# Half of a filter's rows transposed by DMA instead of on TensorE, with a new order of the work

## The chip, the cores and the metric

The kernel runs on one core of one Trainium2 chip. The metric is the device time of one execution in microseconds (us). A core has five engines that run side by side and wait for one another through semaphores: TensorE (PE in the profile; PEld are its weight loads), VectorE (DVE), ScalarE (ACT), GpSimd (POOL) and SyncE (SP). SP and ScalarE also issue DMAs, each into a queue of its own, and 16 DMA engines serve them.

## What is computed

Sequence length S = 2048, width D = 512, inner width 1792, all in bf16. In short:

```
xn = layernorm(A_q)                                  # over the 512 columns
kv = causal_shift_conv(A_k, A_shift_k, 4 taps) * A_v
y  = irfft(rfft(pad(kv)) * rfft(pad(A_ssm_k)))[:S] + kv * A_ssm_D      # a long convolution along the sequence
s  = xn * y
h  = gelu(xn @ w_gate) * (xn @ w_up)
g  = silu(h @ w_down)
out = A_q + s * g
```

A_ssm_k is the filter: 512 rows (one for each column of the sequence) of 2048 taps.

## The kernel before

**The parts of the work.** The layer norm works on 16 row tiles of 128 rows, four to a quarter q = 0 to 3 (`ln`, L809): statistics on VectorE (L811, L812), the power on GpSimd (L821, L822), the normalisation to XN on VectorE (L825). XN is transposed to xnT, for q = 0 and 1 on TensorE (L844, then a copy out of PSUM), for q = 2 and 3 by one DMA transpose each, issued by SP (L836). The gated product runs in units (`unit`, L1065): for quarter q and block m of 14, a gate piece (4 matmuls of 512 columns with Wg) and an up piece (4 with Wu), GELU on ScalarE (L1093), product HT on VectorE (L1096). The down products (`down`, L1099) follow with Wd. Nearly all matmuls go through one helper, L609.

**The long convolution** is a Fourier transform in two stages by matmul. Stage 1 multiplies with the table F1 along the 128 partitions; the result is staged in SBUF, written to a DRAM scratch (ZH for the filter, ZK for kv) and read back in another order (BH, BK) for stage 2, which works in blocks of 32x32 (L984). The products of the two spectra go through the inverse (ZI, BI, "y"). The filter reaches stage 1 like this: its 512 rows are loaded in four pieces h0 to h3 of 128 rows into Hn; `h_transpose` (L860) turns each piece by eight TensorE transposes of pairs of bf16 taken as fp32 (L868), in two halves of four, and ScalarE or VectorE copies each half to HTr; VectorE adds A_ssm_D to the first row (`h_fold`, L882); `stage1` (L905) multiplies, eight steps u = 0 to 7 of 512 columns twice (for u of 4 and more the first of them in halves of 256 columns, `half1`, L895, so that it can begin before h2 and h3 are there). The staging of stage 1 lies in free parts of XN and X, and ScalarE issues the eight stores to ZH, 512 KB each.

**The shift convolution** of A_k (`kshift`, L944) is a chain on VectorE, four rounds of eight operations over 128x2048 elements (L961, L965, L967, L969); each round ends with kv in V. Before it, GpSimd spreads the taps (SKB, L942).

**What sets the order.** All of this is cut into numbered tasks, in the order in which the code creates them. A list written out by hand, SEQ (L27), names every task once, and the instructions are emitted in just this order: on each engine and in each DMA queue, work is done in the order of the list. Semaphore waits come from the tracker (`Trk`, L82), where tiles overlap. The planner's constants (`Sched`, L292: durations, landing times) only choose PSUM banks and staging slots. ORDER (L26) is the order in which the load tasks are created; the order in which SP issues them is again that of SEQ. Gate and up tiles together hold at most four PSUM banks (NF_BANKS, L51). TensorE begins with 11 matmuls on zeros (`warm_up`, L665).

Read through the numbering, SP issues the loads in this order before the change: x rows 0 and 1 of the 16 row tiles (256 KB), h0, h1, x rows 2 and 3, first gate weights, first up weights, h3, second gate weights, x rows 4 to 7, h2, halo of A_k, second up weights, taps, last weights, k0, last up, third weights, k1, v0, both halves of Wd, v3, k2, v2, k3, v1. The weights come in pieces for m = 0 and 1, 2 to 5, 6 to 9, 10 to 13.

Of the kernel before, what the change touches and what calls it, by code (L numbers as in the profile page):

```python
# [14 lines left out]
DM = 512  # L15
# [10 lines left out]
ORDER = "x00 h0 h1 x01 w0 w1 h2 h3 D0 w2 s0 k0 v0 x1 w3 k1 v1 d0 d1 k2 v2 k3 v3 x2 x3"  # L26
SEQ = (  # L27
    "0 2 3 5 4 7 17 18 6 11 1 8 9 12 10 66 19 67 68 74 20 69 75 50 21 49 52b 13 22 76 83 87b 77 54 56b 132 51 84 133 53 70 88 71 55 125 113 111 134 "
    "135 78 126 72 362 370 26 73 112b 79 372 371 363 364 127 85 80 61 81 86 62 23 373 36 365 14 15 96 452 446 450 448 25 89 90 31 97 64 128 114 447 "
    "453 449 451 378 390 366 374 376 392 368 382 375 58 367 454 60 377 369 16 57 386 115 24 30 384 59 63 388 391 383 387 455 458 393 385 456 457 389 "  # L30
    "380 116 142 141 379 459 129 32 381 37 34 130 33 27 38 131 418 414 422 140 139 416 424 143 420 463 144 65 145 461 136 460 415 417 146 28 39 29 "
    "419 410 137 98 138 464 412 465 117 99 423 402 101 406 421 100 102 408 407 398 462 35 41 42 46 43 44 147 151 148 425 409 149 394 411 400 466 91 "
    "399 413 92 404 152 401 395 118 93 396 119 94 467 103 120 403 121 469 104 45 40 153 397 154 405 155 106 495 491 468 108 497 107 493 105 109 150 "
    "156 122 471 496 511 223 470 123 95 513 224 218 512 499 159 157 498 160 514 161 225 441 442 443 492 158 162 219 110 124 494 220 226 473 501 82 "
    "233 500 436 437 475 163 502 164 167 227 48 177 221 477 234 235 438 483 236 165 228 426 485 222 237 229 47 175 176 230 231 427 476 168 166 243 "
    "169 478 244 170 245 428 246 171 479 238 444 239 481 172 472 474 507 240 173 429 439 509 174 431 430 440 432 445 433 253 232 247 183 178 241 434 "
    "254 242 255 508 510 256 487 257 489 248 249 488 250 515 637 435 490 179 251 180 252 188 480 503 484 181 182 184 258 505 639 635 640 633 636 638 "
    "482 634 185 545 546 543 641 504 519 186 643 644 544 506 642 486 645 520 516 521 517 271 528 189 523 529 284 190 193 187 518 522 259 260 263 524 "
    "530 646 547 549 548 191b 261 262 192 198 297 272 276b 273 533 525 285 264 550 289 265 526 531 534 286b 535 266 551 267 269 536 270 268 538 527 "
    "274 532 553 552 555 554 275 537 539 194 540 541 195 659 196 661 663 664 556 665 667 660 277 287 542 278 288 662 290 669 279 282 280 651 668 675 "  # L40
    "291 310 197 292 203 666 653 283 295b 670 293 647 655 298 649 302 657 299b 656 648 705 650 658 199 677 200 652 573 201 575 296 294 565 676 202 "
    "323 654 709 678 593 311 574 566 300 312b 576 301 303 315 567 204 595 205 206 577 594 304 561 568 596 305 306 609 308b 611 610 579 563 612 313 "
    "601 603 562 578 324 602 695 208 207 314 564 316 307 309 281 325 328 317 604 580 697 569 326 327 209 210 211 329 581 570 597 330 571 599 318 321 "
    "572 319b 598 585 336 213 349 212 331 334 587 600 583 557 696 332b 698 337 582 558 341b 333 338 322 559 339 560 340 586 214 683 588 584 342 343 "
    "320 215 605 606 607 335 216 685 699 217 589 608 344 345 701 591 347b 590 684 686 592 350 613 691 346 354 348 693 671 614 351b 352 623 672 615 "
    "353 355 356 673 357 358 713 717 674 360b 359 618 700 619 624 625 620 616 361 626 621 617 622 627 711 723 628 629 692 694 702 740 630 679 680 631 "
    "632 721 712 687 724 681 703 714 682 725 689 726 707 733 704 719 715 706 688 708 710 768 741 720 734 730 727 716 778 690 772 722 718 742 747 731 "
    "748 749 728 776 770 732 774 773 779 769 735 754 750 743 755 756 761 736 729 762 771 777 744 775 751 752 753 763 737 757 745 738 746 739 758 759 "
    "764 765 766 760 767 "
# [3 lines left out]
LOAD_NS = {("x0_", 262144): 800.0, 262144: 850.0, 524288: 1350.0, ("x", 524288): 2100.0, ("h", 524288): 1400.0, ("wg", 524288): 1550.0, ("wu", 524288): 1450.0, 917504: 2620.0, ("sk", 524288): 1500.0, 344064: 1250.0, 46080: 350.0, 3072: 100.0, 1024: 200.0}  # L53
# [238 lines left out]
class Sched:  # L292
# [8 lines left out]
    FIRST = {"loads": 300.0, "SP": 30500.0}  # L301
    DRAIN = 121.0
    EARLY, TAKEN, SHARED, WAIT = (2500.0, 1.6), 1400.0, 46000.0, 3300.0
    LANDS = (3850.0, 5450.0, 7050.0, 8650.0, 9600.0, 10450.0)
# [94 lines left out]
def build_kernel(nc, A_q, A_k, A_v, A_shift_k, A_ssm_k, A_ssm_D, B_w_gate, B_w_up, B_w_down, out):  # L399
    with ExitStack() as es0:  # L400
# [19 lines left out]
        X = new("X", [128, NT, DM], BF16)  # L420
        XN = new("XN", [128, NT, DM], BF16)
# [35 lines left out]
        HTr = at("HTr", [128, NT // 2, 2 * DM], BF16, kk_at - 16384)  # L457
# [21 lines left out]
        ast = {"H": [T[:, 4 * j:4 * j + 4, :].rearrange("p (r c) d -> p r c d", c=2) for T in (XN, X) for j in (2, 3)], "K": [AST[:, j, :, :, :] for j in range(2)] + [ASX[:]]}  # L479
# [48 lines left out]
        R_AST = {x: [res(f"AST{x}{j}", a) for j, a in enumerate(ast[x])] for x in "HK"}  # L528
# [9 lines left out]
        R_HTr = [[res(f"HTr{t}_{k}", HTr[:, t, 256 * k:256 * (k + 1)]) for k in range(KD)] for t in range(NT // 2)]  # L538
# [17 lines left out]
        R_Z = {"H": [trk.free_res(f"ZH{t}") for t in range(NT // 2)],  # L556
# [9 lines left out]
        pAST = {x: Pool_("AST" + x, len(ast[x])) for x in "HK"}  # L566
# [57 lines left out]
        bHTr = [[B(f"HTr{k}_{h}") for h in range(2)] for k in range(KD)]  # L624
# [4 lines left out]
        bZ = {x: [B(f"Z{x}{i}") for i in range(16 if x == "I" else 8)] for x in "HKI"}  # L629
# [134 lines left out]
        def load_x0(t, ring):  # L764
            load(f"x0_{t}", X[:, 2 * t:2 * t + 2, :], x_dr[:, 2 * t:2 * t + 2, :], R_X[2 * t:2 * t + 2], bX[0][2 * t:2 * t + 2], 262144, ring)

# [32 lines left out]

        for what in ORDER.split():  # L800
            if what[0] in "xa" and len(what) == 3:
                load_x0(int(what[2]), "SP" if what[0] == "x" else "ACT")
                continue
            {"k": load_k, "v": load_v, "w": load_w, "x": load_x, "d": load_wd, "h": lambda i: load_h(i, "SP"), "s": load_taps, "D": load_d}[what[0]](int(what[1:]))
# [4 lines left out]
        def ln(q):  # L809
# [3 lines left out]
            for h in range(1 if q else 4):  # L813
# [10 lines left out]
                for t in range(ts.start, ts.stop):  # L824
                    op([("DVE", 420.0)], lambda e, hd, t=t: hd.tensor_scalar(XN[:, t, :], X[:, t, :], mv[:, t, 0:1], mv[:, t, 3:4], ALU.subtract, ALU.mult),  # L825
                       r=[bX[q][t % 4], b], w=[bXN[t]], rr=[R_X[t], R_mv[t]], ww=[R_XN[t]])
# [51 lines left out]
        for k in range(KD):  # L878
            h_transpose(k)
# [25 lines left out]
        def stage1(x, u, Z):  # L905
            a = B(f"A{x}{u}", pAST[x])
            af = [] if x == "H" else s1_tasks["H"] + kshift_tasks[:1] + [t_table]
            for i in range(2):
                if x == "H" and i == 0 and u >= 4:
                    for k in range(2):  # L910
                        half1(u, k, a)
# [331 lines left out]
```

## Time and profile before

| | us |
|---|---|
| median of 3 runs | 196.24 |
| lowest, highest | 195.81, 196.43 |
| span of the profiled execution, first to last instruction | 193.8 |
| around the span, by the median | 2.4 |

The profile's own execution has only its span on the page; what lies around it is taken from the median of the runs. Of the span, DMA reads of HBM are 27.4 MB and writes 14.7 MB. The costliest groups are the gate, up and down matmuls (55.5, 55.8 and 52.7 us); the 32 transposes of the filter (L868) have 5.0 us of modelled, overlapping time.

How to read the lines that follow: in a timeline, the first number is the start in us, the second the length, then the engine, the line, the operation, what it writes and reads, and how many; in brackets stands how long the engine had been idle and what ended that. Matmuls are pipelined: one of 512 columns is listed with 379 ns, but the next starts 216 ns later. Engine names with a q (SPq) are issuing instructions.

### The profile page before, as it was taken

Reading aid. Unit: us, or ns where it says so; the run is one execution under the profiler, and the core shown is the slowest. Engines: PE = TensorE matmul, PEld = TensorE weight load, DVE = VectorE, ACT = ScalarE, POOL = GpSimd, SP = SyncE. Lnnn points to the kernel's source line nnn. Section 1 sums busy time; section 2 is a strip of 40 time slices with the busy share of each in tenths; the row PEclk is TensorE's granted clock in tenths of the full one; section 3 lists DMA queues with packets and bytes.
Section 4 is the critical chain, followed back from the end, with each engine's and each line's share of the span. In section 5 each row is a group of like instructions: output and inputs, shape, how many; then the busy total and the mean of one; then the engine's idle time right before and its main releaser. Section 6 shows DMA issues by size and latency. Waiting matters only on the chain.

```text
span 193.8 us, 3522 instructions
## 1 busy us (share of the span) xinstructions
PE 189.6 (98%) x1393; PEld 87.0 (45%) x1393; DVE 160.6 (83%) x246; ACT 120.7 (62%) x168; POOL 12.6 (7%) x32
## 2 busy tenths in 40 slices
PE   7999999999999999999999999999999999999993
PEld 2777444444444444443334334343344444444442
DVE  6998899899989797987996697887796871579984
ACT  5789877598794797874578666668656622150031
POOL 5322400000000000020200000000000000000000
PEclk9999999999999999999999999999999999999999
DMA  6999999999575659999999927788244305938643
GB/s 177 335 376 300 357 376 392 405 386 368 239 222 164 211 142 288 386 296 278 305 326 208 318 88 230 260 276 271 110 166 162 108 3 171 369 88 278 231 166 108
DMA packets 34502, 48.14 MB, mean 248 GB/s; under 512 B 8499, under 2 KB 27191, under 8 KB 34486
## 3 DMA queue, kind: packets, MB, share of 16 engines
q1 hardware_dynamic: 28982, 39.53, 63.1%
q10 hardware_dynamic: 5504, 8.39, 11.8%
q8 instruction: 11, 0.18, 0.4%
q14 instruction: 5, 0.04, 0.1%
HBM read 27.39 MB, written 14.68 MB: 217 GB/s over the span
## 4 chain that ended last, share of the span: by engine, by line
PE 94%; DVE 2%; DMA 2%; POOL 0%; ACT 0%; issue 0%
PE psall L609 86%; PE psall L984 5%; DMA X<-in_A_q_dram 2%; PE psall L868 1%; PE psall L844 1%; DVE XN L825 0%; DVE stats L811 0%; DVE HTr L603 0%; POOL mv L822 0%; DVE G L1131 0%; DVE G L1130 0%; ACT G L1128 0%; DVE xnT L603 0%; POOL mv L821 0%; DVE mv L812 0%
## 5 line engine op out<-in xcount | busy, mean ns | idle before, releaser
L609 PE MATMUL psall<-xnT,Wu 128*128 128x512 bf16 (+1 forms) x232 | 55.8, 372 | 0.0
L609 PE MATMUL psall<-xnT,Wg 128*128 128x512 bf16 (+1 forms) x232 | 55.5, 372 | 0.0
L609 PE MATMUL psall<-Wd,HT 128*128 128x512 bf16 (+2 forms) x238 | 52.7, 367 | 0.0
L1096 DVE TENSOR_TENSOR HT<-psall,GE 128x512 bf16<-128x512 f32 x54 | 36.2, 684 | 11.9 <-PE psall L609 10.9
L1093 ACT ACTIVATE GE<-psall 128x512 bf16<-128x512 f32 x54 | 31.2, 601 | 11.3 <-PE psall L609 9.0
L609 PEld LDWEIGHTS psall<-Wd,HT 128*128 128x128 bf16 x238 | 22.1, 98 | 26.2 <-issue 1.9
L609 PEld LDWEIGHTS psall<-xnT,Wg 128*128 128x128 bf16 x232 | 22.1, 98 | 25.8 <-issue 1.8
L609 PEld LDWEIGHTS psall<-xnT,Wu 128*128 128x128 bf16 x232 | 21.9, 98 | 25.7 <-issue 2.1
L600 ACT ACTIVATE HS<-psall 128x1024 bf16<-128x1024 f32 x15 | 14.7, 1022 | 5.2 <-PE psall L984 5.2
L600 ACT ACTIVATE BO<-psall 128x1024 bf16<-128x1024 f32 x10 | 10.0, 1023 | 10.6 <-PE psall L984 10.5
L600 ACT ACTIVATE KB<-psall 128x1024 bf16<-128x1024 f32 x10 | 10.0, 1023 | 7.7 <-PE psall L984 7.7
L965 DVE TENSOR_TENSOR KTM<-KK,SKB 128x2048 bf16<-128x2048 bf16 x12 | 14.6, 1214 | 0.1
L967 DVE TENSOR_TENSOR KAC<-KAC,KTM 128x2048 bf16<-128x2048 bf16 x12 | 14.6, 1213 | 0.0
L600 ACT ACTIVATE AST<-psall 128x1024 bf16<-128x1024 f32 x12 | 12.1, 1021 | 2.4 <-PE psall L609 2.1
L1120 ACT ACTIVATE G<-psall 128x512 bf16<-128x512 f32 x12 | 7.0, 599 | 10.4 <-PE psall L609 9.9
L1122 DVE SCALAR_TENSOR_TENSOR G<-G,psall 128x512 bf16<-128x512 bf16 x12 | 7.9, 683 | 6.3 <-ACT G L1120 6.3
L1047 DVE TENSOR_TENSOR HS<-KB,HS 128x1024 bf16<-128x1024 bf16 x16 | 10.8, 683 | 1.1 <-ACT KB L600 1.0
L603 DVE CAST BO<-psall 128x1024 bf16<-128x1024 f32 x6 | 7.3, 1225 | 5.3 <-PE psall L984 5.2
L1128 ACT ACTIVATE G<-psall 128x512 bf16<-128x512 f32 (+2 forms) x5 | 2.5, 511 | 14.1 <-PE psall L609 14.1
L811 DVE BATCH_NORM_STATS2 stats<-X 128x6 f32<-128x512 bf16 x16 | 10.4, 675 | 0.7 <-DMA X<-in_A_q_dram 0.7
L1047 DVE TENSOR_TENSOR HW<-KB,HW 128x1024 bf16<-128x1024 bf16 x16 | 10.8, 682 | 0.0
L600 ACT ACTIVATE XN<-psall 128x1024 bf16<-128x1024 f32 (+1 forms) x10 | 8.4, 856 | 2.9 <-PE psall L609 2.8
(81 smaller groups left out, 179.4 us busy)
## 6 DMA issues: line engine op xcount, KB each, us to landing
BH<-ZH SPq DMA_DIRECT2D x8, 512.0 KB, 5.8
HW<-HS SPq DMA_DIRECT2D x16, 256.0 KB, 3.0
BK<-ZK SPq DMA_DIRECT2D x8, 512.0 KB, 5.9
ZI<-BO ACTq DMA_DIRECT2D x16, 256.0 KB, 2.5
BI<-ZI SPq DMA_DIRECT2D x8, 512.0 KB, 4.5
ZK<-AST SPq DMA_DIRECT2D x6, 512.0 KB, 3.0
Hn<-in_A_ssm_k_dram SPq DMA_DIRECT2D x4, 512.0 KB, 6.4
KK<-in_A_k_dram SPq DMA_DIRECT2D x4, 512.0 KB, 10.8
```

Source lines behind the costliest of these rows:

```text
L600: return h.activation(o, i, ACTF.Copy, scale=scale)
L603: return h.tensor_copy(o, i)
L609: return h.matmul(o, lhsT=l, rhs=r, start=st, stop=sp)
L811: t_stats[t] = op([("DVE", 670.0)], lambda e, h, t=t: h.bn_stats(stats[:, t, :], X[:, t, :]), r=[bX[q][t % 4]], w=[bst[t]], rr=[R_X[t]], w ...
L965: op([("DVE", dur)], lambda e, h, j=j, m=m: h.tensor_tensor(KTM[:, m.slot, :, :], kk(j), sk(j), ALU.mult), r=need + [bSKB[j], a], w=[m], r ...
L967: op([("DVE", dur)], lambda e, h, m=m: h.tensor_tensor(KAC[:, a.slot, :, :], KAC[:, a.slot, :, :], KTM[:, m.slot, :, :], ALU.add), r=[m], ...
L984: trk.op("PE", lambda h: h.matmul(ps(s, i)[b, :], lhsT=wt(col)[a, :], rhs=data(col)[a, :], start=n < 16, stop=n >= len(todo) - 16, tile_po ...
L1047: return hd.tensor_tensor(o, flat(KB, kb[h]), o, ALU.mult)
L1093: op([("ACT", act(512))], lambda e, h: h.activation(GE[:, g.slot, :], bank(pg), ACTF.Gelu_apprx_tanh), r=[pg], w=[g], rr=lambda: R_bank(pg ...
L1096: op([("DVE", dve(512, 1))], lambda e, h: h.tensor_tensor(HT[:, q % 2, m, :], bank(pu), GE[:, g.slot, :], ALU.mult), r=[pu, g], w=[bHT[q][m]],
L1120: op([("ACT", act(n))], lambda e, h, g=g, pc=pc: h.activation(g, pc(), ACTF.Tanh, scale=0.5), r=[p], w=[bt], rr=lambda p=p: R_bank(p), ww= ...
L1122: op([("DVE", dve(512, 1))], lambda e, h, g=g, pc=pc: h.scalar_tensor_tensor(out=g, in0=g, scalar=1.0, in1=pc(), op0=ALU.add, op1=ALU.mult ...
```

## The change

Rows 256 to 511 of the filter (h2, h3) are no longer turned on TensorE. GpSimd copies them, in four pieces of 128x1024, into HP so that the taps of one stage-1 column lie together; two DMA transposes, issued by SP, then write HTD. HTr shrinks to h0 and h1. Stage 1 of the filter is split by the source: "H" from HTr, "J" from HTD, each with eight steps of 2 matmuls of 512 columns (H still in halves for u of 4 and more). Each has its staging (now in X, and for J also in G) and its eight stores to ZH, of 256 KB with runs of 512 bytes; ScalarE issues those of H, SP those of J. The fold of A_ssm_D is split likewise, 256 columns on HTr and 256 on HTD. Some waits follow from where the new tiles lie: HP and HTD use space of HT, XN and a staging tile.

The first load of x is cut: rows 0, 1 and then 2 and 3. SEQ is new from end to end, and so are some constants of the planner. Read through the numbering, SP issues now: x row 0, x row 1, h0, x rows 2 and 3, first gate weights, first up weights, h1, second gate weights, x rows 4 to 7, second up weights, halo, third gate and up weights, A_ssm_D, taps, k0, h2, k1, last gate and up weights, h3, v0, v3, **DMA transpose 0, DMA transpose 1**, k2, both halves of Wd, v1, a table transpose (MI), k3, v2. The list gives GpSimd its copies in the order h2 (half 1), h2 (half 0), h3 (half 0), h3 (half 1). VectorE begins: statistics of row 0, of row 1, normalisation of row 0, statistics of row 2, normalisation of row 1. TensorE begins: warm-up, eight transposes of h0, first transpose of xn, a stage-1 half, second transpose of xn, three stage-1 halves, first gate and up halves (m = 1), third transpose of xn, a gate half (m = 0), fourth transpose of xn, four transposes of h1, an up half, four transposes of h1, the first wide gate (m = 3). Stage 1 of "J" comes later, between gate, up and down pieces of the first two quarters.

```diff
-ORDER = "x00 h0 h1 x01 w0 w1 h2 h3 D0 w2 s0 k0 v0 x1 w3 k1 v1 d0 d1 k2 v2 k3 v3 x2 x3"
+ORDER = "x01 h0 x11 h1 x22 w0 w1 h2 h3 D0 w2 s0 k0 v0 x1 w3 k1 v1 d0 d1 k2 v2 k3 v3 x2 x3"
...
-    FIRST = {"loads": 300.0, "SP": 30500.0}
+    FIRST = {"loads": 1050.0, "SP": 30500.0}
...
-        HTr = at("HTr", [128, NT // 2, 2 * DM], BF16, kk_at - 16384)
+        HTr = at("HTr", [128, NT // 2, DM], BF16, kk_at - 16384)
+        HP = at("HP", [128, NT, 2, 128], BF16, kk_at - 8192)
+        HTD = at("HTD", [128, NT, 2, 128], BF16, xn_at + 8 * 1024)
...
+        ast = {"H": [quarter(X, j) for j in (8, 10, 12, 14)], "J": [quarter(T, j) for T, j in ((X, 12), (X, 14), (G, 4), (G, 6))],
...
-        def load_x0(t, ring):
-            load(f"x0_{t}", X[:, 2 * t:2 * t + 2, :], x_dr[:, 2 * t:2 * t + 2, :], R_X[2 * t:2 * t + 2], bX[0][2 * t:2 * t + 2], 262144, ring)
+        def load_x0(t, n, ring):
+            load(f"x0_{t}", X[:, t:t + n, :], x_dr[:, t:t + n, :], R_X[t:t + n], bX[0][t:t + n], 131072 * n, ring)
...
-        for k in range(KD):
+        for k in range(2):
             h_transpose(k)
+        h_perm, h_dtr = [], []
+        d_htd = [dsem(f"d_htd{hf}") for hf in range(2)]
+        for hf in range(2):
+            for k in range(2):
+                h_perm.append(op([("POOL", 1250.0)], lambda e, h, hf=hf, k=k: h.tensor_copy(HP[:, 8 * hf:8 * hf + 8, k, :], Hn[:, 2 + k, :].rearrange("p (a t) -> p t a", t=NT)[:, 8 * hf:8 * hf + 8, :]),
+                                 r=[bHn[2 + k]], w=[bHP[hf]], rr=[R_Hn[2 + k]], ww=[R_HP[hf]]))
+        for hf in range(2):
+            def dtr(e, hf=hf):
+                o = HTD[:, 8 * hf:8 * hf + 8, :, :].rearrange("p t k d -> p (t k) d")
+                trk.dma("SP", lambda h: h.dma_start(out=o, in_=HP[:, 8 * hf:8 * hf + 8, :, :].rearrange("p t k a -> p (t k a)"), transpose=True), d_htd[hf], r=[R_HP[hf]], w=[R_HTD[hf]])
+            h_dtr.append(S.add([("loads", 4500.0)], dtr, r=[bHP[hf]], w=[bHTD[hf]], nbytes=W_XT))
...
-        h_fold = op([("DVE", 420.0)], lambda e, h: h.tensor_tensor(HT0, HT0, Drow[:], ALU.add),
-                    r=[bHD, *[bHTr[k][0] for k in range(KD)]], w=[bFold], rr=[R_D, *R_HTr[0]], ww=R_HTr[0])
+        op([("DVE", 420.0)], lambda e, h: h.tensor_tensor(HT0, HT0, Drow[:, 0:256], ALU.add),
+           r=[bHD, *[bHTr[k][0] for k in range(2)]], w=[bFold], rr=[R_D, *R_HTr[0]], ww=R_HTr[0])
+        op([("DVE", 420.0)], lambda e, h: h.tensor_tensor(HD0, HD0, Drow[:, 256:512], ALU.add),
+           r=[bHD, bHTD[0]], w=[bFoldD], rr=[R_D, R_HTD[0]], ww=[R_HTD[0]])
...
+        def stage1_h(x, u):
+            a = B(f"A{x}{u}", pAST[x])
+
+            def st(e):
+                dst = bass.AP(ZH, 4 * u * DM + (256 if x == "J" else 0), [[32 * DM, 128], [DM, 4], [1, 256]])
+                dma(e, dst, ast[x][a.slot].rearrange("p r c d -> p (r c) d"), d_ast[x][a.slot], [R_AST[x][a.slot]], [R_Z["H"][u + (8 if x == "J" else 0)]])
...
+                if x == "H":
+                    data, rd, bd = HTr[:, u, :], R_HTr[u], [bHTr[k][u // 4] for k in range(2)] + ([bFold] if u == 0 else [])
+                else:
+                    data, rd, bd = HTD[:, 2 * u:2 * u + 2, :, :].rearrange("p t k d -> p (t k d)"), [R_HTD[u // 4]], [bHTD[u // 4]] + ([bFoldD] if u == 0 else [])
...
+            zh_tasks[x].append(S.add([("ACT", 350.0) if x == "H" else ("SP", ISSUE)], st, r=[a], w=[bZ["H"][u + (8 if x == "J" else 0)]], nbytes=1.05 * SMALL))
...
-        for t in x_late:
-            S.behind(t, zh_tasks)
+        S.behind(x_late[0], zh_tasks["H"])
+        S.behind(x_late[1], zh_tasks["H"] + zh_tasks["J"])
...
-            af = (down_tasks[q - 2] if q >= 2 else []) + (s1_tasks["H"] if q == 1 else [])
+            af = (down_tasks[q - 2] if q >= 2 else []) + ((s1_tasks["H"] if m < 8 else h_dtr) if q == 1 else [])
```

The new SEQ, a list of 788 task numbers, is told above as far as the text needs it.

## The prediction

> **What bounds the kernel now.** I read the page first: the busy shares, then the slices.
>
> ```profile
> span 193.8 us, 3522 instructions
> ...
> PE 189.6 (98%) x1393; PEld 87.0 (45%) x1393; DVE 160.6 (83%) x246; ACT 120.7 (62%) x168; POOL 12.6 (7%) x32
> ...
> PE   7999999999999999999999999999999999999993
> ...
> DMA  6999999999575659999999927788244305938643
> ```
>
> TensorE (PE) has work in every slice but the first and the last, so the time is its start, plus its work, plus its gaps. The DMA engines are full in slices 1 to 9 (5 to 48 us), while the inputs come in. The chain of waits is TensorE alone from 8.02 to 190.03 us, and it shows the pieces that the change takes out (columns: start, length, what):
>
> ```profile
> 11.97 0.49 PE psall L868 x4
> ...
> 12.69 0.50 PE psall L868 x4
> ...
> 17.52 0.44 PE psall L868 x4
> ...
> 18.40 0.44 PE psall L868 x4
> ```
>
> These are the filter's transposes of h3 and h2. The time outside the span is 196.24 - 193.8 = 2.4 us (2.0 to 2.6 by the three runs); I keep it, so changes of the span are added to the median, 196.24. What this measurement can tell from no change is 0.3%, 0.6 us.
>
> **The change part by part.**
>
> *Transposes gone.* The four groups above: 0.49 + 0.50 + 0.44 + 0.44 = **-1.87 us** on the chain. The stage-1 multiplications of the filter keep their number and widths, so nothing else leaves TensorE. Four evictions of 1.02 us (ScalarE, L600 HTr) go too, and two of 0.68 us move from VectorE to ScalarE. Neither is on the chain: ScalarE is busy 62%.
>
> *New order of the first loads.* The new order gives x row 0, x row 1, h0, x rows 2 and 3, the first gate and up weights, and only then h1. By the landing records of the trace, before has x rows 0 and 1 at 4.35, h0 at 5.59, h1 at 6.87, x rows 2 and 3 at 8.42, the weights at 9.35 and 10.20 us. The bytes up to h0 are the same, so the first transposes again start near 5.7. Rows 2 and 3 took 1.55 us behind h1, and a weight piece of the same size 0.93: they land between 6.5 and 7.2, I take 7.0. There is a catch on VectorE: in the new list the statistics of row 2 stand ahead of the normalisation of row 1, so that one waits for 7.0, then 0.70 (statistics) and 0.41 (L825), and ends at 8.1. The second transpose of xn so starts at about 8.15:
>
> ```profile
> 5.64 1.16 PE L868 MATMUL psall<-ident,Hn 128*128 128x128 f32 x8
> ...
> 8.02 0.40 PE L844 MATMUL psall<-ident,XN 128*128 128x128 bf16 x4
> ```
>
> Before has it at 8.02 and has by then also done four transposes of h1, which after can't have: 0.13 + 0.45 (four at the 0.44 to 0.50 above) = 0.58 lost. Against this, before stops weight loads 0.25 us at 13.38 for the ScalarE copy of the fourth xnT; in the new order rows 2 and 3 come earlier and that copy is done. Net **+0.33 us** (bounds 0 and 1.0). Later weights: up to k0, loads land at 3.15 us per MiB (4.35 to 23.62 us, 6.1 MiB), so the new order brings the weights of the first wide gate, its up and the next pair at about 11.4, 14.6 and 17.2 us. TensorE's work by the rows' lengths reaches them at 12.2, 15.2 and 19.5. Covered, by 0.6 us at the tightest; before's tightest is 0.47 (12.99 landed, 13.46 used).
>
> *GpSimd copies.* Four copies 128x1024. The nearest row is four of 128x512:
>
> ```profile
> 20.79 2.42 POOL L942 COPY SKB<-SKR 128x512 bf16<-128x512 bf16 x4 [2.08 <-DMA SKR<-in_A_shift_k_dram]
> ...
> 22.50 1.17 DVE L825 TENSOR_SCALAR XN<-X,mv 128x512 bf16<-128x512 bf16 x2
> ```
>
> That is 0.605 each, so 1.21 for twice the width and 4.8 us in all, on an engine that is otherwise idle. But look at VectorE's L825: the first of the two took 0.847 (the line's median is 0.409) while the last copy ran; VectorE lost 0.44. The reverse is seen too:
>
> ```profile
> 95.37 0.66 DVE L1047 TENSOR_TENSOR HW<-KB,HW 128x1024 bf16<-128x1024 bf16 x1
> ...
> 95.54 0.58 POOL L821 TENSOR_SCALAR mv<-mv 128x4 f32<-128x4 f32 x1 [11.76 <-DVE mv L812]
> ```
>
> L821 takes 0.24 elsewhere, here it ends 0.09 behind the VectorE operation. So the two hold each other up. By position the copies run from 24 to 33 us (h2 lands at 23.7, h3 near 30), beside the shift chain of L961 to L969, which fills VectorE with operations that read two tiles in SBUF; in before no copy ran beside that chain. Bounds: 0 and 4 x 1.21 = 4.8 us lost on VectorE; I take the row's 0.44 four times, 1.8 us. Who waits: behind the chain stand the HT products (L1096), which free the banks of TensorE. What lag is allowed?
>
> ```profile
> 30.57 1.03 PE L609 MATMUL psall<-xnT,Wu 128*128 128x512 bf16 x4
> ...
> 34.56 1.27 DVE L1096 TENSOR_TENSOR HT<-psall,GE 128x512 bf16<-128x512 f32 x2
> ```
>
> The first of these two products belongs to those four matmuls, and ends at 35.2, 3.6 us behind them, with TensorE not waiting. In the new order the shift chain starts near 23 (before: 24.79), and adding 1.135 per chain operation and 0.605 per product (the steps between their starts in this stretch) puts the products 2.1 to 2.5 us behind without any block. 3.6 - 2.4 = 1.2 us are to spare, so TensorE loses 1.8 - 1.2 = **+0.6 us** (0 to 3.6).
>
> [...]
>
> *The two DMA transposes.* Same shape as xnT's:
>
> ```profile
> 88.72 6.94 SPq L836 DMA_TRANSPOSE xnT<-XN  x1
> ...
> 100.70 4.43 SPq L836 DMA_TRANSPOSE xnT<-XN  x1
> ```
>
> SP is held 4.43 to 6.94 us by each, and they land 7.5 to 8.9 us behind issue. The DMA records show 2048 packets of 256 bytes for each, 3.1 to 4.0 us of all 16 engines. Their data is first used near 48 us (VectorE's fold, then stage 1), and they can be issued at 32: hidden with over 5 us to spare. What they cost is what stands behind them on SP: k2, both Wd pieces, v1, a table transpose, k3, v2. In before the second Wd piece lands at 22.70 + 18.8 = 41.5 and is first needed at 52.8. New: + 2.6 (v3 and k2 ahead of it at 1.3) + 6.2 to 8.0 (transposes) - 1.3 (by then 1.5 instead of 2 MiB of ZH stores) = 49 to 50.8, needed near 53. If SP's hold counted in full, + 13.9 and 2.6, it would be 58 and cost 5 us. I take 51: **0**, with 2 us of cover. The stores of the second half go from ScalarE's queue to SP's, 8 x 0.47 us of issue between 53 and 63 us, where SP waits for data anyway; the first BH load needs them only by 73.
>
> [...]
>
> *Rest.* The folds split in two (0.73 us once, now two shorter), the order behind 80 us keeps the same 24 pieces of 32x32 work between wide ones, and the tail behind the last matmul is the same. I cost these at 0 (-0.2 to +0.4).
>
> Sum: -1.87 + 0.33 + 0.6 + 0 = -0.94; 196.24 - 0.94 = **195.3 us**.
>
> **Rivals.**
> 1. *All of the gain.* Copies fall beside the products, rows 2 and 3 land at 6.5: -1.87, 194.4. For it: only one loss in four copies in the row. Against: VectorE has no idle time from 23.6 to 37 us. 0.13.
> 2. *The gain is swallowed*: TensorE has the transposes' 1.87 us free in 12 to 20 us, where weights come in with 0.6 us of cover, and waits there instead, or at the banks: 195.7 to 196.8, about 196.2. 0.22.
> 3. *Slower: the lock on VectorE.* Place: L961 to L969 beside the copies, 24 to 33 us. If each copy holds a chain operation up for 1.0 us, VectorE loses 4.0 and TensorE 4.0 - 1.2 = 2.8: -1.87 + 0.33 + 2.8 = +1.3, 197.5. It turns the result slower once VectorE loses over 3.3 us. 0.21.
> 4. *Slower: Wd late* behind the transposes on SP, 55.5 instead of 53: -0.94 + 2.5, 197.8. For it: SP's long holds. Against: the engines have queued loads to go on with. 0.12.
>
> **How the numbers follow.** The forecast (194.8 to 195.65) has 0.32. Faster by over 0.3%: 0.32 + 0.13 = 0.45; within: 0.22; slower: 0.33. The range 194.3 to 197.8 leaves out the lowest part of rival 1 (0.05) and the far ends of 3 and 4 (0.12).
>
> **What would show it.** L868 with 16 instead of 32 in the groups; the second xn transpose near 8.15; the first wide gate by 12.2; POOL copies of 1.2 us or longer beside L961 to L969 of over 1.21 us, and TensorE gaps from 26 to 45 us whose releaser is HT; Wd landed before 53; the fold not waiting. I am wrong if the copies take much longer than 1.21 each, or if TensorE waits for a landing anywhere behind 12 us.

## The result, and the profile after

| | before | after |
|---|---|---|
| median, us | 195.98 (5 runs) | 201.07 (5 runs) |
| lowest, highest | 195.81, 196.43 | 199.90, 202.13 |
| ratio to before, 95% interval | | 1.0256 (1.0225 to 1.0288) |
| span of the profiled execution | 193.8 | 200.3 (its time: 202.13) |

The change made the kernel slower by 5.1 us; 195.3 was forecast, with a range up to 197.8. Ratios leave out executions more than 1.5% above the fastest of their kernel, three of six in experiment 9 and two of six in experiment 10; medians are of all. In the kernel after, the lines are numbered anew: L618 is the matmul helper, L1005 to L1013 the shift chain (L961 to L969 before), L1140 the product HT, L894 the GpSimd copies, L899 the DMA transposes, L854 the transposes of xn, L878 those of h.

The page of after: busy times, then two of the slices.

```profile
span 200.3 us, 3498 instructions
...
PE 190.8 (95%) x1365; PEld 85.7 (43%) x1377; DVE 165.8 (83%) x244; ACT 119.2 (60%) x167; POOL 24.5 (12%) x36
...
PE   8899988499999999999999999999999999999994
...
PEclk9999999669999999999999999999999999999999
```

TensorE had work in every slice before; now slice 8 (35 to 40 us) has a hole, and in slices 8 and 9 it was granted less than its full clock. GpSimd is busy 24.5 us and not 12.6, VectorE 165.8 and not 160.6. The waits of TensorE name the hole (columns: us in total, times, longest):

```profile
PE psall L618 <- DVE HT L1140: 3.4, 1, 3.4
...
PE psall L854 <- DVE HT L1140: 0.7, 1, 0.7
```

TensorE waits 4.05 us (3.38 + 0.67) for products HT of VectorE. Why they are late is seen when VectorE's timeline and GpSimd's are laid side by side. First the chain in before, then both engines in after:

```profile
24.79 1.21 DVE L961 TENSOR_TENSOR KAC<-KK,SKB 128x2048 bf16<-128x2048 bf16 x1
25.93 1.21 DVE L965 TENSOR_TENSOR KTM<-KK,SKB 128x2048 bf16<-128x2048 bf16 x1
```

```profile
25.02 3.03 DVE L1009 TENSOR_TENSOR KTM<-KK,SKB 128x2048 bf16<-128x2048 bf16 x1
27.97 0.68 DVE L1140 TENSOR_TENSOR HT<-psall,GE 128x512 bf16<-128x512 f32 x1
28.57 2.46 DVE L1011 TENSOR_TENSOR KAC<-KAC,KTM 128x2048 bf16<-128x2048 bf16 x1
30.96 0.68 DVE L1140 TENSOR_TENSOR HT<-psall,GE 128x512 bf16<-128x512 f32 x1
31.56 2.45 DVE L1009 TENSOR_TENSOR KTM<-KK,SKB 128x2048 bf16<-128x2048 bf16 x1
33.93 3.03 DVE L1005 TENSOR_TENSOR KAC<-KK,SKB 128x2048 bf16<-128x2048 bf16 x1
36.89 0.68 DVE L1140 TENSOR_TENSOR HT<-psall,GE 128x512 bf16<-128x512 f32 x1
37.49 1.21 DVE L1011 TENSOR_TENSOR KAC<-KAC,KTM 128x2048 bf16<-128x2048 bf16 x1
```

```profile
24.93 5.02 POOL L894 COPY HP<-Hn 128x1024 bf16<-128x1024 bf16 x2
30.17 5.71 POOL L894 COPY HP<-Hn 128x1024 bf16<-128x1024 bf16 x2 [0.23 <-DMA Hn<-in_A_ssm_k_dram]
```

While GpSimd copies (24.93 to 29.95, 30.17 to 35.88), the four chain operations take 3.03, 2.46, 2.45 and 3.03 us; once it is done, 1.21 again. By the single records the two engines take turns: the copies end at 26.97, 29.95, 32.93 and 35.88, the chain operations at 28.05, 31.03, 34.01 and 36.97, each 1.08 or 1.09 us behind the copy before it, and each copy but the first 1.87 to 1.90 us behind the chain operation before it. A product HT, which reads one tile in SBUF and one in PSUM, keeps its 0.68 us beside a copy. So VectorE loses 3.03 + 2.46 + 2.45 + 3.03 - 4 x 1.21 = **6.1 us** on the chain.

The hole then has a price of its own. Eight up matmuls in before, TensorE's timeline in after, and two stretches of after with the clock behind the busy times of PE, PEld, DVE, ACT and POOL (0.97 and 0.52; then the DMA engines' share and GB/s):

```profile
37.70 1.89 PE L609 MATMUL psall<-xnT,Wu 128*128 128x512 bf16 x8
```

```profile
33.86 0.38 PE L618 MATMUL psall<-HTr,F 128*128 128x512 bf16 x1
37.62 0.61 PE L618 MATMUL psall<-HTr,F 128*128 128x512 bf16 x1 [3.38 <-DVE HT L1140]
38.03 3.62 PE L618 MATMUL psall<-xnT,Wu 128*128 128x512 bf16 x8
```

```profile
34.00:37.00 3.00, 0.24 (x2) 0.00 (x0) 3.00 (x3) 0.22 (x1) 1.88 (x1) 0.97 1.09 214
37.00:44.00 7.00, 6.38 (x16) 2.38 (x17) 5.76 (x7) 2.71 (x4) 0.00 (x0) 0.52 0.99 213
```

Eight up matmuls that take 1.89 us elsewhere take 3.62: the granted clock was 0.5 for 6.83 us, from 36.83 to 43.66. The five executions of after differ in just this: spans of 198.1 us at a mean clock of 1.000, of 199.0, 199.3 and 199.3 at 0.990 or 0.991, of 200.3 at 0.983. By these five, a mean clock of 0.990 or 0.991, which is 3.6 to 4.0 us at half clock (twice the missing share of the span), goes with 0.9 to 1.2 us more of span, 0.983, the 6.83 us of the trace, with 2.2. The profiled execution alone gives more: TensorE doesn't wait between 37.62 and 43.66 us, so half of these 6.04 us, 3.0, is what the half clock adds there.

The rest of the change, in after's timelines of TensorE and SP:

```profile
6.90 0.39 PE L854 MATMUL psall<-ident,XN 128*128 128x128 bf16 x4
...
8.26 0.40 PE L854 MATMUL psall<-ident,XN 128*128 128x128 bf16 x4
...
12.49 1.68 PE L618 MATMUL psall<-xnT,Wg 128*128 128x512 bf16 x9
```

```profile
32.95 4.91 SPq L899 DMA_TRANSPOSE HTD<-HP  x2
...
38.97 1.04 SPq L590 DMA_DIRECT2D Wd<-in_B_w_down_dram  x2
```

The second transpose of xn starts at 8.26 (8.15 forecast), the first wide gate at 12.49 (by 12.2). The two DMA transposes hold SP for 2.86 and 1.95 us, landed at 37.97 and 40.23, and no instruction waited for them; Wd, behind them, landed at 47.1 and 50.1.

The account for the profiled execution, against the span of before (200.3 - 193.8 = +6.5): -1.87 transposes, +0.8 start (worked out in experiment 6), +4.05 waits for HT, +3.0 clock, and 0.5 not assigned. It is more than the 5.1 between the medians, because this execution is the slowest of the five, with 6.83 us at half clock where the median one (0.991) has some 3.6, and the profiled one of before was a little faster than its median.

### The profile page after: what moved, and what is told of

It is laid out like the page before. It is cut to its first block, busy times and chain, and to the rows that moved or that the text cites. A ratio compares the mean times of both kernels' runs of the same rounds, so it can differ in the third digit from the quotient of the medians.

```text
span 200.3 us, 3498 instructions
## 1 busy us (share of the span) xinstructions
PE 190.8 (95%) x1365; PEld 85.7 (43%) x1377; DVE 165.8 (83%) x244; ACT 119.2 (60%) x167; POOL 24.5 (12%) x36
## 4 chain that ended last, share of the span: by engine, by line
PE 79%; DVE 7%; SPq 5%; DMA 4%; issue 3%; ACT 0%; DVEq 0%
PE psall L618 74%; SPq L590 5%; PE psall L1028 5%; DMA KK<-in_A_k_dram 4%; DVE KAC L1005 2%; DVE KTM L1009 2%; DVE KAC L1011 1%; DVE HT L1140 1%; DVE G L1175 0%; DVE G L1174 0%; ACT G L1172 0%; DVE HTr L904 0%; DVE HT L1130 0%; DVE XN L835 0%; DVEq L173 0%
## 5 line engine op out<-in xcount | busy, mean ns | idle before, releaser
L618 PE MATMUL psall<-xnT,Wu 128*128 128x512 bf16 (+1 forms) x232 | 57.5, 382 | 0.0
L618 PE MATMUL psall<-xnT,Wg 128*128 128x512 bf16 (+1 forms) x232 | 56.5, 377 | 0.0
L618 PE MATMUL psall<-Wd,HT 128*128 128x512 bf16 (+2 forms) x229 | 50.9, 366 | 0.7 <-issue 0.3
L1140 DVE TENSOR_TENSOR HT<-psall,GE 128x512 bf16<-128x512 f32 x54 | 36.6, 683 | 10.5 <-PE psall L618 10.2
L618 PEld LDWEIGHTS psall<-xnT,Wu 128*128 128x128 bf16 x232 | 22.3, 100 | 27.2 <-issue 5.0
L618 PEld LDWEIGHTS psall<-Wd,HT 128*128 128x128 bf16 x238 | 22.4, 98 | 26.0 <-issue 1.3
L618 PEld LDWEIGHTS psall<-xnT,Wg 128*128 128x128 bf16 x232 | 22.0, 99 | 26.4 <-issue 3.2
L1009 DVE TENSOR_TENSOR KTM<-KK,SKB 128x2048 bf16<-128x2048 bf16 x12 | 17.6, 1470 | 0.1
L609 ACT ACTIVATE X<-psall 128x1024 bf16<-128x1024 f32 (+1 forms) x17 | 13.8, 825 | 4.2 <-PE psall L618 4.2
L1011 DVE TENSOR_TENSOR KAC<-KAC,KTM 128x2048 bf16<-128x2048 bf16 x12 | 15.8, 1320 | 0.1
L609 ACT ACTIVATE BO<-psall 128x1024 bf16<-128x1024 f32 x9 | 9.1, 1023 | 6.9 <-PE psall L1028 6.9
L612 DVE CAST BO<-psall 128x1024 bf16<-128x1024 f32 x7 | 8.6, 1223 | 4.5 <-PE psall L1028 4.5
L821 DVE BATCH_NORM_STATS2 stats<-X 128x6 f32<-128x512 bf16 x16 | 10.6, 676 | 1.2 <-DMA X<-in_A_q_dram 1.2
L831 POOL TENSOR_SCALAR mv<-mv 128x1 f32<-128x1 f32 (+1 forms) x7 | 2.0, 281 | 72.6 <-DVE mv L822 72.6
```

The lines of the kernel that those rows point to most:

```text
L609: return h.activation(o, i, ACTF.Copy, scale=scale)
L612: return h.tensor_copy(o, i)
L618: return h.matmul(o, lhsT=l, rhs=r, start=st, stop=sp)
L821: t_stats[t] = op([("DVE", 670.0)], lambda e, h, t=t: h.bn_stats(stats[:, t, :], X[:, t, :]), r=[bX[q][t % 4]], w=[bst[t]], rr=[R_X[t]], w ...
L1009: op([("DVE", dur)], lambda e, h, j=j, m=m: h.tensor_tensor(KTM[:, m.slot, :, :], kk(j), sk(j), ALU.mult), r=need + [bSKB[j], a], w=[m], r ...
L1011: op([("DVE", dur)], lambda e, h, m=m: h.tensor_tensor(KAC[:, a.slot, :, :], KAC[:, a.slot, :, :], KTM[:, m.slot, :, :], ALU.add), r=[m], ...
```

## The experiments

Theory L: the copies and the chain hold each other up, and that is the slow-down. Rival Q: SP's queue, with the transposes and what stands behind them. Rival O: the new order itself. The expectations call Q "Rival S". Ratios are to runs of before on the same chip. The diffs are shortened, with `...` for what is left out, and give changes of SEQ in words.

**1. No copies.** Each copy is cut to one element, and the DMA transposes read Hn as it is, so the filter's second half is in a wrong order of taps; all else as in after. (So the transposes are issued from 24.1 us on and not from 32.95; the loads behind them come at the same time, Wd lands at 46.7 and 49.6, in after at 47.1 and 50.1.)

```diff
-h.tensor_copy(HP[:, 8*hf:8*hf+8, k, :], Hn[:, 2+k, :].rearrange("p (a t) -> p t a", t=NT)[:, 8*hf:8*hf+8, :])
+h.tensor_copy(HP[:, 8*hf, k, 0:1], Hn[:, 2+k, 0:1])
-h.dma_start(out=o, in_=HP[:, 8*hf:8*hf+8, :, :].rearrange("p t k a -> p (t k a)"), transpose=True)
+h.dma_start(out=o, in_=Hn[:, 2+hf, :], transpose=True)
```

> The changed kernel with the four GpSimd copies of 128x1024 cut to one element each; the two DMA transposes read h2 and h3 as they were loaded, so the filter's rows 256 to 511 enter stage 1 with their taps in the wrong order (this part of the computation is changed). All else, the order of the work too, is as in the changed kernel. Theory L (the copies and the shift chain on VectorE exclude each other): every operation of the chain back at 1.21 us, no TensorE pause at 34 us (3.4 us) and none at 28 us (0.7), TensorE clock granted 1.0 all along; 196.0 - 1.87 + 0.8 (later start) = 194.9 us, 194.5 to 195.6. Rival S (the DMA transposes on SP, and the loads behind them, cost the time): 198 to 201 us, pauses that end with a DMA landing. Rival O (the new order itself is worse): 198 to 201 us, pauses spread over the span.

Measured: 195.28 us, ratio 0.9972 (0.9947 to 0.9996); profiled span 193.3, clock 0.999. No wait for HT is left among TensorE's waits, and every chain operation takes 1.20 to 1.23 us from 25 us on. The first of them, and what is left of the new order's waits:

```profile
25.06 1.23 DVE L1009 TENSOR_TENSOR KTM<-KK,SKB 128x2048 bf16<-128x2048 bf16 x1
```

```profile
PE psall L854 <- DVE XN L835: 0.5, 1, 0.5
PE psall L618 <- ACT HTr L609: 0.4, 1, 0.4
```

The copies cost 201.07 - 195.28 = 5.8 us; O and Q can't be the cause, since the order, two such transposes and the loads behind them are all still here. But the gain is 0.5, not 1.87: something else takes part of it.

**2. Two copies.** The copies of half 0 cut to one element, those of half 1 kept; the first transpose reads Hn (wrong order of taps there).

```diff
+h.tensor_copy(HP[:, 8:16, k, :], ...) if hf else h.tensor_copy(HP[:, 0, k, 0:1], Hn[:, 2 + k, 0:1])
...
+in_=HP[:, 8:16, :, :]... if hf else Hn[:, 2, :]
```

> As the run without copies, but the two copies for the second half of the taps are kept, and the second DMA transpose reads them; the first reads h2 as loaded (the filter's taps are changed for that half). Theory L: the chain loses 1.5 us for each copy, 3 us instead of 6.1; TensorE had about 2 us to spare (6.1 lost on VectorE, 4.05 us of pauses), so pauses of about 1 us and no loss of clock: 195.5 to 196.7 us. Rival S or O: as the changed kernel, 198 to 201 us.

Measured: 196.71 us, ratio 1.0058 (1.0039 to 1.0077), span 195.4, clock 1.0.

```profile
PE psall L854 <- DVE HT L1140: 1.1, 1, 1.1
PE psall L618 <- DVE HT L1140: 1.1, 1, 1.1
```

The two chain operations beside the copies took 3.03 and 3.05 us, the others 1.21. Two copies cost 1.4 us, four 5.8: the first two use up what VectorE has to spare, and pauses of 1.1 us cost no clock (1.000).

**3. Copies in the kernel before.** Before, with four GpSimd copies of the same form from Hn into a free staging tile, put beside the chain; nobody reads them.

```diff
+            trk.op("POOL", lambda h: h.tensor_copy(XC[:, 1024 * i:1024 * i + 1024].rearrange("p (t a) -> p t a", a=128), Hn[:, 2 + k, :].rearrange("p (a t) -> p t a", t=NT)[:, 8 * hf:8 * hf + 8, :]), ...)
...
+            for i in extra.get(t.n, ()):
+                xcopy(i)
```

> The kernel before, unchanged in its result, with four more GpSimd copies of 128x1024 with the change's access pattern from h2 and h3 into a tile that is free at that time, queued behind the tap copies; nothing reads them. Theory L: they run from about 23 to 32 us beside the shift chain, which loses 5 to 7 us; TensorE pauses 2 to 5 us, and if one pause is longer than about 3 us its clock falls to half for some 7 us, 3 us more: 198 to 203 us. Rivals S and O: a copy of 1.2 to 1.9 us on an idle engine costs nothing: 195.8 to 196.4 us.

Measured: 200.23 us, ratio 1.0232 (1.0215 to 1.0249), span 198.7, clock 0.990. The copies alone make before slower by 4.5 us. GpSimd's line, and three of VectorE's:

```profile
24.43 11.65 POOL L1196 COPY AST<-Hn 128x1024 bf16<-128x1024 bf16 x4
```

```profile
27.55 3.06 DVE L965 TENSOR_TENSOR KTM<-KK,SKB 128x2048 bf16<-128x2048 bf16 x1
30.53 2.56 DVE L882 TENSOR_TENSOR HTr<-HTr,Drow 1x512 bf16<-1x512 bf16 x1
...
34.73 2.44 DVE L965 TENSOR_TENSOR KTM<-KK,SKB 128x2048 bf16<-128x2048 bf16 x1
```

Even the fold, 512 elements on one partition, read from two tiles in SBUF, takes 2.56 us and not 0.73 as in before. TensorE paused 2.58 us for an HT, up to 34.94, and was granted 0.57 of its clock from 34 to 38 us, some 3.4 us at half. The 3 us that the expectation gave for a pause was the author's estimate from after (a pause of 3.38 us, 6.83 at half clock); here half clock came with 2.58.

**4. Copies on ScalarE.** Same copies, same data, by ScalarE; moved a little later in the order, with k2 and Wd kept behind the transposes on SP. Nothing of the computation is left out.

```diff
-op([("POOL", 1250.0)], ... h.tensor_copy(HP..., Hn...)
+op([("ACT", 1050.0)], ... h.activation(HP..., Hn..., ACTF.Copy)
```

> The changed kernel with the four copies on ScalarE instead of GpSimd, placed in ScalarE's order where h2 and h3 have landed; the transposes and the three loads behind them keep their order on SP and stand some places later in the list. Result unchanged. Theory L: ScalarE shares nothing with VectorE, so the chain is back at 1.21 us; four copies of about 1.05 us fit into ScalarE's idle time: no pause, clock 1.0, 194.8 to 195.8 us, 0.1 to 0.6% below the kernel before. Rival S or O: 198 to 201 us.

Measured: 199.85 us, ratio 1.0212 (1.0187 to 1.0238), span 198.0, clock 1.0. The expectation failed by 4 us. Three views: the copies, the chain (both with minimum, median and maximum in ns behind the colon), TensorE's waits.

```profile
L873 ACT ACTIVATE HP<-Hn x4: 2081/2104/2141, 28.1 to 36.3; 128x1024 bf16<-128x1024 bf16 x4
```

```profile
L988 DVE TENSOR_TENSOR KTM<-KK,SKB x12: 1203/1215/1226, 25.4 to 73.5; 128x2048 bf16<-128x2048 bf16 x12
```

```profile
PE psall L597 <- ACT xnT L588: 2.4, 1, 2.4
PE psall L597 <- ACT X L588: 2.2, 2, 1.9
```

The chain is undisturbed beside ScalarE's copies, with a median of 1.215 us where operations beside GpSimd's took 2.45 to 3.03. But a copy takes 2.1 us here as well, and stands in ScalarE's queue ahead of the evictions for which TensorE waits: 4.6 us more than without copies, and 2.4 + 2.2 of waits. (Some tasks moved as well; the run doesn't separate that.) Pauses of 2.4 and 1.9 us cost no clock: it was full (0.998 to 1.0) in all four executions.

**5. Three forms of the copy.** In before, later on, 1024 elements copied by GpSimd and by ScalarE from Wd, not read: as in after (reading every 16th element, writing dense), reading runs of 8 and writing every 128th, and plain (forms 1, 2 and 3).

```diff
+                o, c = o.rearrange("p (t a) -> p t a", a=128), SRC.rearrange("p (a t) -> p t a", t=NT)[:, 0:8, :]
...
+                o, c = o.rearrange("p (t a) -> p a t", a=128), SRC.rearrange("p (a t) -> p a t", t=NT)[:, :, 0:8]
...
+                c = SRC[:, 0:1024]
```

> The kernel before with three extra copies of 128x1024 each on GpSimd and on ScalarE, at about 160 us, where VectorE has little to do; nothing reads them. Forms, in this order: reading every 16th element as the change does and writing in a row; reading runs of 8 and writing with a step; plain. From the runs so far: a GpSimd copy of the first form takes 1.88 us from the release by VectorE to its end, a ScalarE one 2.10. Theory R (the step of 32 bytes in reading is what costs): GpSimd 1.9, then 1.2 and 1.2 us; ScalarE 2.1, then 1.05 and 1.05. Rival (the time next to the shift chain was longer than the copy itself): GpSimd 1.2 and ScalarE 1.05 in all forms. Time of the whole kernel: no more than 3 us above the kernel before, from the extra ScalarE work.

Measured: one execution, 203.34 us, span 201.5. Forms 1, 2 and 3 took 2.06, 4.75 and 1.06 us on ScalarE, 2.04, 5.23 and 1.46 on GpSimd (there beside VectorE, so upper values); the lines hold them in the order of their size:

```profile
L1202 POOL COPY AST<-Wd x3: 1463/2041/5226, 97.4 to 104.2; 128x1024 bf16<-128x1024 bf16 x3
L1202 ACT ACTIVATE AST<-Wd x3: 1057/2060/4751, 170.2 to 177.1; 128x1024 bf16<-128x1024 bf16 x3
```

VectorE worked beside the copies of GpSimd there, and its timeline shows two more that were held up (a single L1047 takes 0.68 elsewhere, an L825 0.40; the last column but the brackets is how many a line sums up):

```profile
98.30 1.69 DVE L1047 TENSOR_TENSOR HS<-KB,HS 128x1024 bf16<-128x1024 bf16 x1
...
100.51 5.92 DVE L825 TENSOR_SCALAR XN<-X,mv 128x512 bf16<-128x512 bf16 x4
```

On ScalarE the price of a copy is in its pattern: 1.06 us plain, 2.06 when each read steps 32 bytes, 4.75 when each write steps 256. Forms 1 and 3 came out on ScalarE as expected, form 2 did not. The whole kernel lost 7.5 us in this one execution, where 3 at most were expected: TensorE paused 3.5 us for a G behind the held L825, its mean clock was 0.992, some 3.2 us at half, and ScalarE's 7.9 us stood ahead of its last evictions.

**6. No copies, row 1 ahead of row 2.** As experiment 1, with the statistics of row 2 moved behind the normalisation of row 1 in SEQ.

```diff
- ... stats 2, pow 1, stage-1 half, XN 1 ...
+ ... pow 1, stage-1 half, XN 1, stats 2 ...
```

> As the run without copies (the filter's taps of rows 256 to 511 in the wrong order), and in VectorE's order the normalisation of x row 1 now stands ahead of the statistics of x row 2. That run was 0.5 us below the kernel before, where 1.87 - 0.33 = 1.5 was forecast. Theory St (the new start loses the rest: TensorE waits 0.47 us at 8.2 us for the normalisation of row 1): the second transpose of xn moves from 8.2 to about 7.7 us and the time falls by 0.3 to 0.5 us, to 194.7 to 195.0 us. Rival: the transposes of rows 2 and 3 or the weights then wait instead, same time as without the exchange, 195.2 us.

Measured: 194.47 us, ratio 0.9931 (0.9913 to 0.9949), span 192.5: 0.8 less than experiment 1.

```profile
7.52 0.39 PE L833 MATMUL psall<-ident,XN 128*128 128x128 bf16 x4
...
12.04 1.14 PE L597 MATMUL psall<-xnT,Wg 128*128 128x512 bf16 x5
```

The second transpose of xn starts at 7.52 (8.21 in experiment 1), the first wide gate at 12.04 (12.44). That is 0.4 us by one task's place; of the rest of the 0.8, another 0.4 is a wait for an eviction to ASX that the trace of experiment 1 has and this one hasn't.

What the whole start costs follows from the work done ahead of the first wide gate, at 13.46 in before. By then before has done eight transposes of the filter more than after (0.94 us, at 0.44 to 0.50 for four) and stage-1 matmuls of 2048 columns more (0.86, at 216 ns for 512). Without these 1.8 us it would stand at 11.66. After stands at 12.49, experiment 1 at 12.44, experiment 6 at 12.04: the new start costs 0.8 us, and 0.4 with row 1 ahead. For experiment 1 that gives -1.87 + 0.8 + 0.4 (the wait for ASX) = -0.7, measured -0.5.

**7. Eight half copies.** After, each copy cut into two of 512 elements.

```diff
+[h.tensor_copy(HP[:, 8*hf+j:8*hf+j+4, k, :], Hn...[:, 8*hf+j:8*hf+j+4, :]) for j in (0, 4)]
```

> The kernel after with each of the four GpSimd copies cut into two of half the size (8 copies of 512 elements per partition, some 0.94 us each, one behind the other); nothing else. Theory L (each copy and each VectorE operation on two SBUF tensors exclude each other, and TensorE's pauses then also cost half-clock time once a pause is long): the time locked away is the same, about 8 x 0.94 = 7.5 us, but one chain operation waits 0.94 us and not 1.9 at a time, so the delay is spread over more operations: TensorE's waits for HT still sum to 3 to 4.5 us, the longest stays under 2.5 us and the half clock goes: 197 to 199 us. If the half clock follows the sum of the waits and not the longest one: 200.5 to 201.5 us, as after. Rival (the copies are slow because VectorE's operations starve them, and short ones slip between): chain operations near 1.5 us, waits under 2 us, 196 to 197 us.

Measured: 201.24 us, ratio 1.0265 (1.0234 to 1.0295), span 199.8, clock 0.991. VectorE's chain and TensorE's waits:

```profile
25.61 2.10 DVE L1009 TENSOR_TENSOR KTM<-KK,SKB 128x2048 bf16<-128x2048 bf16 x1
...
28.23 1.53 DVE L1011 TENSOR_TENSOR KAC<-KAC,KTM 128x2048 bf16<-128x2048 bf16 x1
```

```profile
PE psall L618 <- ACT X L609: 2.5, 1, 2.5
PE psall L618 <- DVE HT L1140: 1.4, 2, 0.8
...
PE psall L854 <- DVE HT L1140: 0.4, 1, 0.4
```

Neither side has it whole, and the time is in the range of neither. The chain is held less, as the rival said: seven operations sum to 11.9 us for 8.5, which fits the estimate of 0.94 us for a half copy, 0.6 of it beside a product; the waits for HT fall from 4.05 to 1.8 us, and no half clock follows them (1.00 from 20 to 60 us). But the last copy ends at 41.0 and not 35.9, and so SP reaches its later work some microseconds later: an eviction to the staging X waits for the store of what lay there before (3.6 us), TensorE waits 2.5 us for that eviction at 61 to 64 us, and some 3.4 us at half clock come with it (0.83 of the clock from 60 to 70 us). The time is that of after by another road; that it equals what was given for a half clock that follows the sum of the waits is chance.

**8. Through DRAM.** No copies: the transposes read Hn, two stores write the block to DRAM in rows of 256 bytes, two loads read it back as 16 rows to a partition; start as in experiment 6. Nothing of the computation is left out.

```diff
+dma("SP", bass.AP(ZT, 128 * k, [[256, 128], [128 * 256, NT], [1, 128]]), HP[:, k, :, :], ...)
...
+dma("SP", HTD[:, 8 * hf:8 * hf + 8, :, :]..., bass.AP(ZT, 2048 * hf, [[4096, 128], [1, 2048]]), ...)
```

> A version without copies on any engine: row 1 ahead of row 2 at the start as in e6; the DMA transposes read Hn as it is, and the order of the rows is put right by writing the transposed block to a DRAM tensor (two stores of 512 KB in rows of 256 bytes) and reading it back as 16 rows per partition (two loads of 512 KB); the stores and loads stand in SP's queue behind the transposes, the loads of k2, d0, d1 and v1 behind them. Output is the reference's. From e6 (194.47): the shift chain stays at 1.21 us an operation and nothing is added to an engine, so 194.3 to 194.9 us if the filter's half is back before its fold at 47.7 us (transposes land at about 38, store 2.5 us, load 3 us: 44) and Wd, issued some 4 us later and so landing at 51 to 54, before its first use at 59.8. Rival (the queue): stores of 256-byte rows take the DMA engines so long that the half comes after 49 us or Wd after 60: each us of it a us of TensorE's wait, 195.5 to 199 us.

Measured: 204.08 us, ratio 1.0414 (1.0380 to 1.0448). The rival held:

```profile
PE psall L598 <- DMA HTD<-ZT: 5.7, 1, 5.7
```

The transposes landed at 38.2 and 42.0, the second store at 46.7, the loads at 52.7 and 54.5, for a use at 48.9. With the wait of 5.7 us come some 6.8 us at half clock (granted: 0.99 from 48 to 52 us, 0.50 to 56, 0.66 to 60). The expectation also took the first use of Wd, 59.8 us, from after, where TensorE is late; in experiment 6 it is at 51.85. Wd, which landed at 57.7 and 60.1 here, would have been too late by itself.

**9 and 10. The same, stage 1 of that half 12 or 20 tasks later.** Also the load of k2 ahead of the stores. (A task whose buffer isn't free yet is passed over until it is.)

```diff
- DMA transposes, stores, k2, loads, Wd, v1; J tasks in place
+ DMA transposes, k2, stores, loads, Wd, v1; J tasks 12 (20) later
```

> The version of e8 mended where its profile showed it late: the load of k2 ahead of the two stores (in e8 it stood between them and the read back), and the 25 tasks of the DMA half's stage 1 (fold, matmuls, evictions, stores) moved 12 tasks later in the one order of all tasks, some 4 groups of matmuls or 3.5 us on TensorE. In e8 the transposes landed at 38.2 and 42.0, the second store at 46.7, the read back at 52.7 and 54.5, and TensorE waited 5.7 us for it and then ran 6.8 us at half clock. Theory (what e8 lost is that wait and its clock and nothing else): the read back lands near 50 to 51, the first such matmul is due at about 51, so no wait or one under 1 us, full clock, 194.5 to 195.5 us. Rival (the filter's spectrum is needed as early as before, so the 3.5 us come back as a wait ahead of the first product with it at 72 to 80 us): 196 to 199 us.

> As e9, with those tasks 20 later and not 12, some 6 us on TensorE. Theory of e9: the read back is in time by a margin, 194.5 to 195.5 us as e9, or a little better if e9 still waits. Rival of e9 (the delay comes back behind): more of it comes back than in e9, 197 to 200 us.

Measured: 210.77 us, ratio 1.0651 (1.0609 to 1.0694), and 211.54 us, 1.0767 (1.0737 to 1.0796); the times of these two scatter more than the others' (207.6 to 214.1; 210.4 to 251.5), so only the waits are read here. First 9, then 10:

```profile
PE psall L604 <- DMA HTD<-ZT: 4.3, 1, 4.3
PE psall L604 <- DMA Wd<-in_B_w_down_dram: 2.3, 1, 2.3
```

```profile
PE psall L604 <- DMA Wd<-in_B_w_down_dram: 7.2, 1, 7.2
```

Both expectations failed. In experiment 9 the stores landed only at 47.1 and 50.4, with k2 in front of them. Wd, which stands behind the read back, landed at 58.8 us and later in both, for a use near 52: TensorE waits for it once it no longer waits for the filter. No version that computes the whole result was faster than before.

## Why the prediction was wrong

The sum was -1.87 + 0.33 + 0.6 + 0 = -0.94; the median moved by +5.1.

- **The step that failed is the GpSimd copies, put at +0.6 us.** It took 1.21 us for a copy, from SKB rows that step 8 bytes in their source, where these step 32: 1.88. And it took 0.44 us lost per copy on VectorE, a row that showed a normalisation partly covered. In its place the runs showed the two engines taking turns (in after a chain operation ends 1.08 or 1.09 us behind a copy, a copy 1.87 to 1.90 behind a chain operation), 6.1 us lost on VectorE and not 1.8, even above the bound of 4.8 (four copies of 1.21); 4.05 us of waits for TensorE (bound: 3.6). The allowance of 1.2 us was of the right size: in experiment 2, 3.7 us lost on VectorE became 2.2 us of waits, in after 6.1 became 4.05. The prediction's own sign of being wrong, copies much longer than 1.21 us, came true.
- Which operations were held is seen in four runs. Alone, a chain operation, which reads two SBUF tiles, takes 1.20 to 1.23 us (experiment 1). Beside GpSimd's copies it took 2.45 to 3.03 (after), and 2.44 and 3.06 (experiment 3); beside ScalarE's copies 1.215 (experiment 4). An HT, with one SBUF input, took its 0.68 beside a GpSimd copy (after). The rows of before were held for less: L825 0.85 us for 0.41, L821 0.58 for 0.24.
- **A term was missing: TensorE's clock behind a pause.** The prediction put it at nothing. It is 0.9 to 1.2 us of span for 3.6 to 4.0 us at half clock by the five executions, and 2.2 for 6.83, which the trace puts at 3.0; one execution of after had none. The rival of the lock (197.5) had mechanism and place right, and lacked the copy's length and the clock. Its turning point, 3.3 us lost on VectorE, fits the one run near it: with 3.7 lost, experiment 2 is 0.9 us slower than before.
- *Transposes gone, -1.87*: consistent with experiment 6, where 0.4 of the start's cost is left: -1.87 + 0.4 = -1.5, measured -1.3 in span and -1.4 between the medians.
- *Start, +0.33 (0 to 1.0)*: mis-sized; it is 0.8. The catch that the prediction named (statistics of row 2 ahead of row 1) was right: the second transpose of xn came at 8.26, 8.15 forecast. The credit of 0.25 for a stop of the weight loads in before was used up by a new stop in after, 0.31 us for the copy of the second xnT:

```profile
9.35 0.33 PEld L618 LDWEIGHTS psall<-xnT,Wg 128*128 128x128 bf16 x4 [0.31 <-ACT xnT L609]
```

- *DMA transposes, 0*: right in time. They landed 4.3 to 5.0 us behind issue, not 7.5 to 8.9, and Wd at 50.1, 51 forecast. After doesn't test the cover of 2 us, since its TensorE first uses Wd at 59.8. Experiment 6 does: Wd landed at 46.9 and 49.9, its first use is at 51.85, and nothing waits; experiments 9 and 10 push Wd to 59 us and later, and TensorE waits.
- *Around the span, 2.4*: 1.7 to 1.9 in every execution of a known time and span. It cancels, since changes were added to the median.

## What to carry to other kernels

Before work goes to an engine that looks idle, ask what it shares with the one beside it: here a GpSimd copy of 1.88 us next to VectorE operations on two SBUF tiles cost VectorE 1.24 to 1.82 us, so its price is that of VectorE's time, not of GpSimd's. Take the length of a copy from a row with the same step in memory, not only the same size (1.21 us by a row that steps 8 bytes, 1.88 measured at 32). Where TensorE is the bound, a pause can cost half clock on top of its length: those of 2.5 to 5.7 us did in the traces of after and of experiments 3, 5, 7 and 8, those of 2.4 us and less in experiments 2 and 4 didn't (next section). And look at what every rerouted byte stands behind in SP's queue.

## What the runs showed of the hardware

- In the trace of after the granted clock was 0.5 from 36.83 to 43.66 us, 6.83 us, with a pause of TensorE of 3.38 us that ended at 37.62. In experiment 3 some 3.4 us at half clock came with a pause of 2.58 us, in 7 some 3.4 with one of 2.51, in 8 some 6.8 with one of 5.69, in 5 some 3.2 (by the mean clock, 0.992) with one of 3.5. None came with pauses of 2.40 and 1.89 us in experiment 4, nor with two of 1.1 us in experiment 2 (both 1.000). Experiments 9 and 10, with waits of 4.3 and 7.2 us for a DMA and several shorter ones, had mean clocks of 0.967 and 0.968.
- The length of a pause alone doesn't give that of the half clock: the pause of 3.5 us in experiment 5 came with some 3.2 us, that of 3.38 in after with 6.83, and other executions of after had none or 3.6 to 4.0 us by their mean clocks (1.000, and 0.990 to 0.991). What decides it is not shown.
- A copy of 1024 bf16 per partition takes 1.06 us plain on ScalarE, 2.06 to 2.14 reading in steps of 32 bytes, 4.75 writing in steps of 256; on GpSimd 1.88 reading in steps of 32 bytes (from the end of the VectorE operation that it waited for).
- A one-input normalisation (L825) was held beside GpSimd copies too: in experiment 5 four of them took 5.92 us beside the copies of 5.23 and 1.46, where one alone takes 0.41 (median in before).
- How long DMA transposes hold SP varies: in experiment 8 the two took 13.3 us of SP from 24.5 us on, the second 4.48 of them from 33.40; in after 4.9, issued at 32.95, when the last earlier load had landed at 32.94. That the loads ahead are the reason is not shown.
